# A planned attention-and-MLP kernel: more buffers lent to the Exp results, and a new plan

## The chip, the cores and the metric

The kernel runs on one core of a Trainium2 chip. The core has engines that work side by side and wait for each other through semaphores: TensorE (PE in the profile; its weight loads are PEld), VectorE (DVE), ScalarE (ACT), GpSimd (POOL) and SyncE (SP), which here issues the transfers. The metric is the device time of one execution in microseconds (us). The kernel before took 1624.14 us, the median of three runs (1622.63 to 1628.64). A further execution of it, which the hardware profiler recorded, took 1620.71 us; its trace spans 1618.9 us. Durations below are from that trace.

## The reference

Two layers are applied twice, with the same weights both times, to x of 2048 tokens by 512 features in bfloat16:

```python
def _A_ref(x, wqkv, wo):                     # 32 heads of 16 features
    qkv = (x @ wqkv) -> q, k, v per head
    p = softmax(q @ k.T * 16 ** -0.5)        # 2048 x 2048 for each head
    return concat_heads(p @ v) @ wo

def _B_ref(x, w1, w2):                       # 512 -> 1792 -> 512
    return silu(x @ w1) @ w2

for _ in range(2):
    x = x + _A_ref(layernorm(x), wqkv, wo)
    x = x + _B_ref(layernorm(x), w1, w2)
```

What costs most is the exponential of the scores: 2 layers x 32 heads x 2048 x 2048 values.

## The kernel before

**Tiles.** The tokens are four chunks c of 512 queries and sixteen blocks kt of 128 keys; the heads are eight head blocks hb of four heads. A segment (class Seg) is one layer, one chunk and one head block over a range of keys. There are 74 of them, numbered 0 to 73. Layer 1 (L = 0 in the code) has segments 0 to 31, all with 16 key blocks. In layer 2 the first two chunks begin before the last chunk of layer 1 has passed its MLP, so their head blocks are split: an "old" segment over the first 12 key blocks (numbers 32 to 41) and a "new" segment over the last 4 (among numbers 42 to 54). The old one's result is kept and is later multiplied by a factor and added to the new one's. A tile is two heads of a segment by one key block: 128 keys x 1024 scores. There are 2048 tiles, in a fixed order.

**What a tile passes through.** PE makes its scores (two products into one of three wide PSUM slots, `scores`). Then one of two ways follows. ACT takes the Exp of the whole tile into a buffer (`act_turn`), and PE multiplies that buffer with V (`values`). Or DVE makes an approximate power of two with one instruction (`dve_turn`, a "pass"), and three shifted copies of its bits are made, on POOL (`pool_turn`) or on DVE; PE then multiplies all four buffers with V. A pass thus takes one Exp off ACT and gives DVE one instruction, POOL or DVE three, and PE three more products with V. The buffers are 14 tiles p0 to p13 and, at times, rows of other tiles that are idle, which the list `lent` adds to the pool for a range of segments.

**Who decides the order.** Class Flow holds a clock for each engine with written-in durations, and steps through the kernel while it is built: at each step the engine that is first free takes its next instruction (`pe_turn`, `act_turn`, `dve_turn`, `pool_turn`). Engines execute in the order so written and do not reorder. Side work is cut into Pieces (K, Q, V, output projection, MLP) with due times. A letter for each 16 tiles (RULES) picks a row of KINDS: how many buffers must be free before a pass is chosen (`spare`), how many shifts may be queued, how hard side work is pushed, and so on; `want_dve` decides whether a tile goes to DVE. Where PE has nothing else and its planned share of the last 3300 ns is below WARM, `warm` issues a product with zero weights whose result adds nothing ("zero product", line 1393), to keep TensorE's clock up.

**The chain ahead of a segment.** Before a segment's first scores its QT must stand: the biased product q_ps on PE (`q_bias`, line 312), then `q_sum` on DVE (line 421). For layer 2's "new" segments a K piece goes ahead: four products, a copy to kq (line 334), `k_out` (line 321), a maximum (line 348) and the bias tile bm (line 412). When a segment ends, `close` copies its accumulated result (lines 1176, 1180 or 1184), a DMA transposes it, and `heads_norm` (lines 513 and 514) divides by the sums. A K or Q piece needs the one narrow PSUM bank, which the piece before it must have left.

Of the kernel before, what the change touches and what calls it, by code (L numbers as in the profile page):

```python
# [12 lines left out]
FP32 = mybir.dt.float32  # L13
# [7 lines left out]
def kernel(  # L21
# [14 lines left out]
    S, D = xf.shape  # L36
    F = B_w1.shape[-1]
    P = 128
    H = 32
    DH = D // H  # L40
# [3 lines left out]
    NQC = S // 512  # L44
    FT = F // P
    HB = H // 4
# [3 lines left out]
    VW = DH + 1  # L50
# [109 lines left out]
    E = cpool.tile([P, P], FP32, name="E")  # L160
# [104 lines left out]
    def dve(ns, fn, g=""):  # L265
        return ("dve", ns, fn, g)
# [62 lines left out]
    def k_piece(L, c, hb):  # L329
        cell = {}  # L330

        def out():
            st = cell["st"] = stpool.tile([P, 512], BF16, name="kq", tag="kq")
            nc.vector.tensor_copy(out=st[:], in_=cell["ps"][:, :])  # L334
            move(kept_q[L, hb, c, :, :], st[:])

        p = Piece(four(
            lambda cts: k_mm(c, hb, cell["ps"][:, :], cts),
            lambda: bank(cell, "k_ps"),
        ) + [dve(700, out, "c"), dve(302, lambda: k_out(c, hb, cell["st"][:]), "l")])  # L340
        p.key = (L, c, hb)
        p.store = Piece([])
        return p
# [163 lines left out]
        return fetch, f  # L507


    def heads_norm(at_ps, hb, attn):  # L510
        n = at_ps.shape[2]
        rec = bmpool.tile([P, 4, 8, 1], FP32, name="rec", tag="rec")[:, :, 0:n, :]
        nc.vector.reciprocal(rec, at_ps[:, :, :, DH : DH + 1])
        nc.vector.tensor_tensor(
            out=attn[:, :, 64 * hb : 64 * hb + DH * n].rearrange("p t (j d) -> p t j d", j=n),
            in0=at_ps[:, :, :, 0:DH],
            in1=rec.to_broadcast([P, 4, n, DH]),
            op=ALU.mult,
        )

# [2 lines left out]
    def heads_piece(oT, seg, attn):  # L523
        alone = seg.c < 2 and (seg.L == 1 or seg.hb < 2)
        alone = alone or (seg.L, seg.c, seg.hb) == (1, NQC - 1, HB - 2)
        k = 0 if alone else seg.hb % 2
        if k == 0:
            at_cell["at"] = opool.tile([P, 4, 2, P], BF16, name="at", tag="at")
        at = at_cell["at"]
        turn(at[:, :, k, :], oT[:])  # L530
        if not alone and k == 0:
            return None
        n = 4 * (k + 1)
        heads = at[:].rearrange("p t s (j w) -> p t (s j) w", j=4)[:, :, 0:n, :]
        return Piece([dve(640 if k == 0 else 920, lambda: heads_norm(heads, seg.hb - k, attn))])

    def o_transpose(a_ps, attn, tq):
        for ct in range(CT):
# [61 lines left out]
    def ffn_pieces(c, emit_out, ln, after):  # L600
# [33 lines left out]
            ))  # L634
        return pieces

    normed = {}

    def next_pieces(c, L, ln, after):
        ln = ln_pieces(c, ln, after)  # L640
        v = [v_piece(4 * c + tq, L) for tq in range(4)]
        normed[c] = ln[-1]
        v[0].after = [ln[-1]]
        return ln + v

    def tail_mm(slots, tq, k):
# [7 lines left out]
    def ending(oT, attn, slots, units):  # L654
# [27 lines left out]
        heads_norm(at_ps, hb, attn)  # L682
# [244 lines left out]
    done = n_old + 2 + 2 * HB  # L927
    keyed = max(s.i for s in segs if s.kind == "new" and s.c == 0) + 1
    lent = [
        (0, HB, spare(rows(x_flat, 0, 3))),  # L930
        (0, 2 * HB, spare(rows(x_flat, 3, 5))),
        (0, 3 * HB, spare(rows(x_flat, 5, 7))),
        (0, 4 * HB, spare(rows(x_flat, 7, 8))),
        (n_old + 3, n_old + HB, spare(idle_hidden)),
        (n_old + 4, 99, spare(wv_rows)),
        (keyed, 99, spare(key_rows)),
        (done, 99, spare(rows(v_flat, 0, 8))),
    ]

    class Flow:  # L940
# [36 lines left out]
        def rule(self, n):  # L977
            letter = RULES[n // STRETCH]
            (
                self.spare, self.many, self.few, self.behind, self.hurry, self.help, self.wait,  # L980
            ) = KINDS[letter]

        def landed(self, at):
# [184 lines left out]
        def close(self):  # L1168
# [17 lines left out]
            self.o_free = self.dve + 50  # L1186
            self.close_at = None
            self.open += 1
            if self.open == len(segs):
                return oT  # L1190
            if oT is not None:
# [54 lines left out]
            return max(self.end + 916 * (j + 1), t.at + 490 + 1017) + 50  # L1246

        def want_dve(self, t, at, two):
            if not two or t.n < 4 or t.n - self.last_dve < 2:
                return False  # L1250
            left = 2 * len(t.seg.kts) - 2 * (t.kt - t.seg.kts[0]) - t.pr
            if left < LAST or len(self.zs) > 0 or len(self.passes) > self.behind:
                return False
            if sum(b[0] <= at + 600 for b in self.bufs) - self.owed() < self.spare:
                return False
            if sum(len(l) for l in self.lanes) > ROWS:
                return False
            return self.dve < at + 475 + LATE
# [362 lines left out]
    KINDS = {  # L1621
# [10 lines left out]
    }  # L1632
# [161 lines left out]
```

## Time and profile before

| what | value |
|---|---|
| median of three runs | 1624.14 us (1622.63 to 1628.64) |
| profiled execution | 1620.71 us, span 1618.9 us |
| ACT | 1557.0 us busy, 1596 Exps in the flow |
| PE | 1546.3 us busy (matmul latency counted in) |
| DVE, POOL | 1239.8 us and 1293.6 us busy |
| DVE passes (line 1531) | 452 |
| zero products in the flow (line 1393) | 211 |
| granted TensorE clock, mean | 0.991 |

A busy PE in such a page is not a PE at its peak: a product's latency is counted with it, and 383 ns stand for one that others overlap. ACT's Exps overlap as well (a mean of about 1200 ns each, issued less than that apart), so its busy time is the time in which at least one ran. The line numbers are those of the kernel before.

### The profile page before, as it was taken

To read this page: it belongs to the slowest core of one execution; us is meant where nothing else is said; L and a number is where in the kernel's file an instruction comes from. 1 tells how busy PE (TensorE), PEld (TensorE's weight loads), DVE (VectorE), ACT (ScalarE), POOL (GpSimd) and SP (SyncE) were. 2 spreads that over 40 slices of the span, in tenths; PEclk is the share of its full clock that TensorE was granted. 3 is DMA by queue.
4 is the path that set the end of the run, shared out by engine and by line. 5 is a ranking of instruction groups with operands and counts; after the bars stand their busy time and mean duration, and the time that the engine had idled before them with its cause. 6 is when DMAs were issued, how large, how long until landed. Compare 5 with 4: busy or idle time off the path is not lost.

```text
span 1618.9 us, 41459 instructions
## 1 busy us (share of the span) xinstructions
PE 1546.3 (96%) x16750; PEld 477.4 (29%) x16756; DVE 1239.8 (77%) x1550; ACT 1557.0 (96%) x1767; POOL 1293.6 (80%) x1349
## 2 busy tenths in 40 slices
PE   8999999999999999999999999998999999999998
PEld 3322222233322323233222232222223222222333
DVE  7898888876777678658987668886878887777764
ACT  6999999999999999999999998998999999999993
POOL 3899998987898778868777866876879998889880
PEclk9999999999999999999999999998999999999999
DMA  5011101100210011001120011112100110010000
GB/s 195 21 40 37 30 23 27 27 11 11 37 23 11 11 27 41 11 14 33 57 59 23 14 27 35 37 35 45 30 11 17 33 27 14 18 33 18 17 24 14
DMA packets 105744, 49.24 MB, mean 30 GB/s; under 512 B 79024, under 2 KB 105040, under 8 KB 105552
## 3 DMA queue, kind: packets, MB, share of 16 engines
q1 hardware_dynamic: 103536, 45.51, 11.0%
q8 instruction: 131, 2.15, 0.6%
q10 hardware_dynamic: 2016, 1.08, 0.2%
q14 instruction: 61, 0.50, 0.1%
HBM read 17.20 MB, written 11.27 MB: 18 GB/s over the span
## 4 chain that ended last, share of the span: by engine, by line
PE 59%; ACT 22%; DVE 11%; issue 6%; POOL 2%; DMA 1%; ACTq 0%; DVEq 0%; POOLq 0%
PE slot L1282 21%; PE q_ps L1358 19%; ACT p L1497 15%; PE y_ps L312 7%; PE h_ps L312 4%; DVE p L1531 3%; ACT v L1497 3%; ACT t_sb L580 2%; PE k_ps L312 2%; PE v_ps L312 1%; PE q_ps L312 1%; POOL p L1592 1%; DVE hT L584 1%; PE w_ps L1393 1%; DVE kq L334 1%
## 5 line engine op out<-in xcount | busy, mean ns | idle before, releaser
L1497 ACT ACTIVATE p<-slot 128x1024 bf16<-128x1024 f32 x1168 | 1172.4, 1203 | 17.4 <-PE slot L1282 17.1
L1592 POOL TENSOR_TENSOR p<-p,steps 128x512 int32<-128x512 int32 x681 | 710.9, 1068 | 186.6 <-DVE p L1531 167.2
L1282 PE MATMUL slot<-QT,KT 32*128 32x512 bf16 x4096 | 596.6, 383 | 36.8 <-ACT p L1497 18.3
L1358 PE MATMUL q_ps<-p,v 128*17 128x512 bf16 x4956 | 566.1, 384 | 5.6 <-DVE p L1531 2.3
L1531 DVE TENSOR_SCALAR p<-slot 128x1024 uint16<-128x1024 f32 x341 | 415.5, 1219 | 106.0 <-PE slot L1282 99.9
L1282 PEld LDWEIGHTS <-KT 32*128 32x128 bf16 x4096 | 198.8, 91 | 615.9 <-issue 609.9
L1497 ACT ACTIVATE v<-slot 128x1024 bf16<-128x1024 f32 x289 | 329.3, 1211 | 1.9 <-PE slot L1282 1.9
L1358 PEld LDWEIGHTS <-v 128*17 128x17 bf16 x6808 | 157.3, 88 | 292.9 <-issue 244.1
L1358 PE MATMUL q_ps<-v,v 128*17 128x512 bf16 x1222 | 195.2, 382 | 1.2 <-POOL v L1592 0.8
L1592 POOL TENSOR_TENSOR v<-p,steps 128x512 int32<-128x512 int32 x159 | 170.4, 1081 | 23.2 <-DVE p L1531 17.1
L1592 POOL TENSOR_TENSOR p<-v,steps 128x512 int32<-128x512 int32 x123 | 130.8, 1081 | 8.4 <-DVE v L1531 8.0
L312 PE MATMUL h_ps<-xnT,w_sb 128*32 128x512 bf16 x1568 | 130.3, 384 | 6.8 <-DVE hT L584 6.6
L312 PE MATMUL y_ps<-w_sb,hT 128*32 128x512 bf16 x1568 | 121.8, 383 | 0.5 <-DVE hT L584 0.5
L584 DVE SCALAR_TENSOR_TENSOR hT<-t_sb,h_ps 128x512 bf16<-128x512 f32 x98 | 66.8, 682 | 58.2 <-ACT t_sb L580 57.9
L1531 DVE TENSOR_SCALAR v<-slot 128x1024 uint16<-128x1024 f32 x69 | 84.2, 1220 | 26.8 <-PE slot L1282 25.7
L1497 ACT ACTIVATE wkq<-slot 128x1024 bf16<-128x1024 f32 x74 | 87.2, 1215 | 0.1
L312 PE MATMUL k_ps<-xnT,wkq 128*32 128x512 bf16 x960 | 78.2, 383 | 0.0
L580 ACT ACTIVATE t_sb<-h_ps 128x512 f32<-128x512 f32 x98 | 76.0, 776 | 0.0
L421 DVE SCALAR_TENSOR_TENSOR QT<-qc,cols,q_ps 128x512 bf16<-128x512 bf16 x74 | 55.0, 743 | 21.6 <-PE q_ps L312 21.0
L1358 PE MATMUL q_ps<-wkq,v 128*17 128x512 bf16 x336 | 58.3, 387 | 0.6 <-ACT wkq L1497 0.4
L312 PEld LDWEIGHTS <-hT 128*32 128x32 bf16 x2016 | 41.0, 95 | 57.1 <-issue 40.8
L1497 ACT ACTIVATE wv_sb<-slot 128x1024 bf16<-128x1024 f32 x44 | 51.7, 1174 | 4.7 <-PE slot L1282 4.5
(168 smaller groups left out, 1469.5 us busy)
## 6 DMA issues: line engine op xcount, KB each, us to landing
qc<-kept_q SPq DMA_DIRECT2D x70, 112.0 KB, 2.0
kept_q<-kq SPq DMA_DIRECT2D x60, 128.0 KB, 1.8
w_sb<-in_B_w_dram SPq DMA_DIRECT2D x2, 1792.0 KB, 13.0
out_dram<-x_sb SPq DMA_DIRECT2D x15, 128.0 KB, 1.7
x_sb<-in_A_x_dram SPq DMA_DIRECT2D x3, 512.0 KB, 7.0
old_q<-QT SPq DMA_DIRECT2D x10, 128.0 KB, 1.7
q_was<-old_q SPq DMA_DIRECT2D x10, 128.0 KB, 2.0
at<-oT SPq DMA_TRANSPOSE x63, 2.3
```

The costliest lines, as they stand in the source:

```text
L312: nc.tensor.matmul(ps[g, :], lhsT=lhsT[:, g], rhs=rhs, start=start, stop=stop, skip_group_check=True)
L334: nc.vector.tensor_copy(out=st[:], in_=cell["ps"][:, :])
L421: nc.vector.scalar_tensor_tensor(out=dst, in0=qc[:], scalar=own, in1=ps, op0=ALU.mult, op1=ALU.add)
L580: nc.scalar.activation(t_sb, ps, ACT.Tanh, scale=0.5)
L584: nc.vector.scalar_tensor_tensor(out=hT[:, ft, :], in0=t_sb, scalar=1.0, in1=ps, op0=ALU.add, op1=ALU.mult)
L1282: nc.tensor.matmul(self.slots[k][:, jj, :], lhsT=KT[32 * j : 32 * j + KR, t.seg.hb, t.kt * P : (t.kt + 1) * P], rhs=t.seg.QT[32 * j : 32 * ...
L1358: nc.tensor.matmul(self.o_ps[32 * j : 32 * j + VW, :], lhsT=vs[seg.L][:, t.kt, 4 * seg.hb + j, :], rhs=buf[:, jj, :], start=not seg.opened ...
L1393: nc.tensor.matmul(out[0:DH, :], lhsT=wkq[rows, 0, 2 * D : 2 * D + DH], rhs=wo_sb[rows, 0, :], start=out is not self.o_ps, stop=out is not ...
L1497: nc.scalar.activation(buf[:].rearrange("p a b -> p (a b)"), self.slots[x.slot][:].rearrange("p a b -> p (a b)"), ACT.Exp, scale=float(SCALE),
L1531: nc.vector.tensor_scalar(out=whole.bitcast(U16), in0=self.slots[x.slot][:].rearrange("p a b -> p (a b)"), scalar1=float(UNIT), scalar2=fl ...
L1592: nc.gpsimd.tensor_tensor(out=b1.bitcast(I32), in0=b0.bitcast(I32), in1=steps32[:, k : k + 1].to_broadcast([P, 512]), op=ALU.add,)
```

## The change

1. **Lent buffers.** Rows of layer 2's V tile (x_flat) are lent during layer 1. Before, three, two, two and one buffers were taken back after segments 7, 15, 23 and 31. After, each chunk's V rows hold two buffers, taken back at segments 12, 20, 28 and 38, and a gate holds that chunk's V pieces until then. Rows of layer 1's V tile, which serve layer 2's kept results, are lent one by one while their result isn't yet written or is already used; before, all were lent from segment 59 on. Idle rows of the MLP's hidden tile are lent until segment 52 instead of 49.
2. **Planned durations ("clocks").** `k_out` is planned at 350 ns instead of 302. `heads_norm` is split into `heads_rec` and `heads_mul`, two steps with durations of their own, between which other work can stand.
3. **Zero products.** WARM goes from 0.65 to 0.70.
4. **Letters.** KINDS gets two more fields (`last`, `solo`, which `want_dve` reads), and RULES is written anew.

```diff
-        ) + [dve(700, out, "c"), dve(302, lambda: k_out(c, hb, cell["st"][:]), "l")])
+        ) + [dve(700, out, "c"), dve(350, lambda: k_out(c, hb, cell["st"][:]), "l")])
...
-        return Piece([dve(640 if k == 0 else 920, lambda: heads_norm(heads, seg.hb - k, attn))])
...
+        return Piece([dve(190 if k == 0 else 280, first), dve(410 if k == 0 else 560, second, "l")])
...
+    wanted = [HB * (c + 1) + HB // 2 for c in range(NQC - 1)] + [NQC * HB + HB - 2]
+    gates = [Piece([]) for c in range(NQC)]
...
-        v[0].after = [ln[-1]]
+        v[0].after = [ln[-1], gates[c]]
...
-        (0, HB, spare(rows(x_flat, 0, 3))),
-        (0, 2 * HB, spare(rows(x_flat, 3, 5))),
-        (0, 3 * HB, spare(rows(x_flat, 5, 7))),
-        (0, 4 * HB, spare(rows(x_flat, 7, 8))),
-        (n_old + 3, n_old + HB, spare(idle_hidden)),
+        *((0, wanted[c], spare(new_v_rows(c))) for c in range(NQC)),
+        *((99, NQC * HB + hb, old_o[hb]) for hb in range(1, HB)),
+        (n_old + 3, keyed - 1, spare(idle_hidden)),
         (n_old + 4, 99, spare(wv_rows)),
         (keyed, 99, spare(key_rows)),
-        (done, 99, spare(rows(v_flat, 0, 8))),
...
+            if self.open in wanted:
+                gate = gates[wanted.index(self.open)]
+                gate.done, gate.ready = True, self.pe
+            if seg.i == NQC * HB - 1:
+                self.bufs += [(self.pe, b) for hb in range(1, HB) for b in old_o[hb]()]
+            if seg.kind == "new" and seg.c == 0:
+                self.bufs += [(self.dve, b) for b in rows(v_flat, seg.hb, seg.hb + 1)()]
...
-            if not two or t.n < 4 or t.n - self.last_dve < 2:
+            if not two and len(self.exps) < self.solo or t.n < 4 or t.n - self.last_dve < 2:
...
-            if left < LAST or len(self.zs) > 0 or len(self.passes) > self.behind:
+            if left < self.last or len(self.zs) > 0 or len(self.passes) > self.behind:
...
-    LAST, ROWS, LATE, EVEN = 5, 20, 900, 0
-    SPAN, WARM = 3300, 0.65
+    ROWS, LATE, EVEN = 20, 900, 0
+    SPAN, WARM = 3300, 0.7
...
-        "bbbbbbbbmmmmmmmmwwwwwwwwwwwwwwwwppppppppbbbbbbbbddddddddcccccccc"
-        "aaaaaaaakkkkkkkknnnnnnnnvvvvvvvvwwwwwwwwwwwwwwwweeeeeeeellllllll"
+        "ggggggggggggggggllllllllaaaaaaaappppppppppppppppdddddddddddddddd"
+        "GGGGGGGGGGGGGGGGkkkkkkkkkkkkkkkknnnnnnnnnnnnnnnnaaaaaaaaaaaaaaaa"
```

No matrix product, Exp or transfer of the mathematics is added or left out; which tiles go to DVE, and the order on each engine, are.

More of the change, by code (lines that the diff above doesn't have):

```diff
@@ L507, in f_piece, with heads_rec, heads_mul @@
         return fetch, f
-    def heads_norm(at_ps, hb, attn):
-        n = at_ps.shape[2]
-        rec = bmpool.tile([P, 4, 8, 1], FP32, name="rec", tag="rec")[:, :, 0:n, :]
+    def heads_rec(at_ps):
+        m, n = at_ps.shape[1:3]
+        rec = bmpool.tile([P, 4, 8, 1], FP32, name="rec", tag="rec")[:, 0:m, 0:n, :]
         nc.vector.reciprocal(rec, at_ps[:, :, :, DH : DH + 1])
+        return rec
+    def heads_mul(at_ps, rec, hb, attn):
+        m, n = at_ps.shape[1:3]
         nc.vector.tensor_tensor(
@@ L516, in heads_norm @@
             in0=at_ps[:, :, :, 0:DH],
-            in1=rec.to_broadcast([P, 4, n, DH]),
+            in1=rec.to_broadcast([P, m, n, DH]),
             op=ALU.mult,
@@ L534, in heads_piece, with first, second @@
         heads = at[:].rearrange("p t s (j w) -> p t (s j) w", j=4)[:, :, 0:n, :]
-        return Piece([dve(640 if k == 0 else 920, lambda: heads_norm(heads, seg.hb - k, attn))])
+        cell = {}
+        def first():
+            cell["rec"] = heads_rec(heads)
+        def second():
+            heads_mul(heads, cell["rec"], seg.hb - k, attn)
+        return Piece([dve(190 if k == 0 else 280, first), dve(410 if k == 0 else 560, second, "l")])
     def o_transpose(a_ps, attn, tq):
@@ L681, in ending @@
         warm(max(0, 5 - len(units[4:])))
-        heads_norm(at_ps, hb, attn)
+        heads_mul(at_ps, heads_rec(at_ps), hb, attn)
         a_ps = gpool.tile([P, 4, P], BF16, name="a4_ps", tag="g")
@@ L925, in key_rows, with new_v_rows @@
         return [wkq[:, ct, 0 : 2 * D].rearrange("p (a b) -> p a b", a=2) for ct in range(CT)]
-    done = n_old + 2 + 2 * HB
     keyed = max(s.i for s in segs if s.kind == "new" and s.c == 0) + 1
+    def new_v_rows(c):
+        return rows(x_flat[:, 4 * H * VW * c : 4 * H * VW * (c + 1)], 0, 2)
+    old_o = [spare(rows(v_flat, hb, hb + 1)) for hb in range(HB)]
     lent = [
-        (0, HB, spare(rows(x_flat, 0, 3))),
-        (0, 2 * HB, spare(rows(x_flat, 3, 5))),
-        (0, 3 * HB, spare(rows(x_flat, 5, 7))),
-        (0, 4 * HB, spare(rows(x_flat, 7, 8))),
-        (n_old + 3, n_old + HB, spare(idle_hidden)),
+        *((0, wanted[c], spare(new_v_rows(c))) for c in range(NQC)),
+        *((99, NQC * HB + hb, old_o[hb]) for hb in range(1, HB)),
+        (n_old + 3, keyed - 1, spare(idle_hidden)),
         (n_old + 4, 99, spare(wv_rows)),
         (keyed, 99, spare(key_rows)),
-        (done, 99, spare(rows(v_flat, 0, 8))),
     ]
@@ L980, in rule @@
                 self.spare, self.many, self.few, self.behind, self.hurry, self.help, self.wait,
+                self.last, self.solo,
             ) = KINDS[letter]
```

21 rows, old and new, of the table KINDS are left out of this document.

## The prediction

> **What bounds the kernel now.** I read the page's engine table first, then the busy time of ACT by stretch, then who ACT waited for, and last the timelines of ACT and DVE around each of its waits.
>
> ```profile
> PE 1546.3 (96%) x16750; PEld 477.4 (29%) x16756; DVE 1239.8 (77%) x1550; ACT 1557.0 (96%) x1767; POOL 1293.6 (80%) x1349
> ...
> PEclk9999999999999999999999999998999999999999
> ```
>
> ACT and PE both stand at 96%. PE's figure counts latency; ACT decides, as the stretches show (start and end, length, ACT busy with its count, granted TensorE clock, DMA share, GB/s):
>
> ```profile
> 240.00:260.00 20.00, 18.48 (x20) 0.91 0.18 40
> 260.00:596.00 336.00, 335.58 (x381) 1.00 0.09 19
> 596.00:610.00 14.00, 12.97 (x15) 0.88 0.17 37
> 610.00:812.00 202.00, 202.00 (x228) 1.00 0.12 30
> ...
> 981.00:1000.00 19.00, 13.60 (x17) 1.00 0.14 41
> ...
> 1066.00:1092.00 26.00, 23.43 (x26) 0.87 0.19 36
> ...
> 1110.00:1142.00 32.00, 25.91 (x29) 0.79 0.22 40
> 1142.00:1540.00 398.00, 396.54 (x453) 1.00 0.10 22
> sum 1500.00, ACT 1477.19; mean ACT 113.63
> ```
>
> From 40 to 1540 us ACT is idle for 22.81 of 1500 us. Where the granted clock is full it hardly rests (0.42 of 336 us, 0 of 202, 1.46 of 398). It rests in four stretches whose clock is below 1.00, and at a few segment starts. The waits of that time go to one place, PE's scores; none goes to a missing buffer (waiter, whom for, us in total, times, longest):
>
> ```profile
> ACT p L1497 <- PE slot L1282: 15.2, 22, 4.0
> ACT wv_sb L1497 <- PE slot L1282: 4.5, 3, 3.5
> ACT v L1497 <- PE slot L1282: 1.9, 5, 0.6
> ```
>
> ACT's timeline has the single waits, in brackets, and the price of an Exp:
>
> ```profile
> 34.58 6.52 ACT L1497 ACTIVATE p<-slot 128x1024 bf16<-128x1024 f32 x7 [0.84 <-PE slot L1282]
> ...
> 813.83 2.85 ACT L1497 ACTIVATE p<-slot 128x1024 bf16<-128x1024 f32 x3 [1.08 <-PE slot L1282]
> ...
> 992.47 1.02 ACT L1497 ACTIVATE p<-slot 128x1024 bf16<-128x1024 f32 x1 [4.02 <-PE slot L1282]
> 999.94 5.61 ACT L1497 ACTIVATE p<-slot 128x1024 bf16<-128x1024 f32 x6 [1.38 <-PE slot L1282]
> ...
> 1121.88 1.02 ACT L1497 ACTIVATE wv_sb<-slot 128x1024 bf16<-128x1024 f32 x1 [3.53 <-PE slot L1282]
> ```
>
> A lone Exp takes 1.02 us and seven take 6.52, so one more costs (6.52 - 1.02) / 6 = 0.917 us. The waits at 813.83, 992.47, 999.94 and 1121.88 are the starts of segments 33, 43, 44 and 54: QT was late. DVE's timeline ahead of two of them:
>
> ```profile
> 983.99 1.22 DVE L1531 TENSOR_SCALAR p<-slot 128x1024 uint16<-128x1024 f32 x1
> ...
> 986.07 1.26 DVE L1565 TENSOR_SCALAR p<-p 128x1024 int16<-128x1024 int16 x1
> ...
> 1120.38 0.75 DVE L421 SCALAR_TENSOR_TENSOR QT<-qc,cols,q_ps 128x512 bf16<-128x512 bf16 x1 [3.41 <-PE q_ps L312]
> ```
>
> At segment 43 a pass and a shift stand in DVE's queue ahead of the K piece and QT; at 54 DVE waits 3.41 us for the biased product, at half the clock.
>
> **The change, part by part.** Counts come from the two programs' order of instructions on each engine.
>
> *Exps and passes.* Passes fall from 452 to 446, so ACT has 1602 Exps for 1596: 6 x 0.917 = **+5.5 us** on the engine that decides. POOL's shifts fall from 1203 to 1179, DVE's rise from 153 to 159, PE's products with V fall from 6808 to 6772. These lie beside ACT (DVE 77%, POOL 80% busy); if that cover went, they would be a gain.
>
> *Lent buffers.* No wait of ACT above is for a buffer, and passes don't rise, so more buffers alone are worth 0. The gate could hold V pieces, and behind them the K pieces of layer 2, but all V pieces stand in the same segments in both orders (16, 23 or 24, 30, 41): 0. If an Exp into a lent row had to wait for that row's last reader it would show as a new wait of ACT; by the list above the old lent rows cost at most 1.9 us in five waits, so 0 to +1.9, and I take 0, since all of those name the scores.
>
> *Late QTs.* I counted how many tiles of scores PE still has to issue after the biased product of the next segment. Most are far ahead; the close ones are the waits. Segment 43 keeps 0 tiles, but between QT of 42 and QT of 43 DVE loses one pass (1.22) and one shift (mean 0.77 in its rows): 2.0 us sooner, and ACT has one more Exp to fill with, so its idle time goes from 4.02 to 4.02 - 2.0 - 0.92 = 1.1: **-2.9**. The bounds are -4.0 (all of it) and 0 (the pass gone, but the K piece as late). Segment 44 likewise loses one pass and gains one Exp, 1.38 - 1.22 - 0.92 is below zero: **-1.4** (0 to -1.4). Segment 54's biased product comes two tiles earlier (0 to 2), and 55's too: 2 x 0.917 = -1.8, with 0.3 for 55: **-2.1** (0 to -3.5). Segment 33 gets worse: a kq copy (0.69), a `close` copy (0.69) and `k_out` (median 0.70) now stand ahead of its QT: **+2.1** on ACT's wait of 1.08 (0 to +2.9, with the K piece's 16 quarter products, 0.87, in full). Segment 2 goes from 1 tile to 0 and segment 73 from 11 to 1; the early segments with 0 (4, 6 and 8) show waits up to 0.3, hence **+0.6** for two (0 to +2.2, with segment 33's 1.08 each).
>
> *Zero products.* They go from 211 to 349. At about 0.22 us each that is 30 us of PE, but they're issued only where the plan has nothing else, and three slots stand between PE and ACT: 0, or up to 0.2 us where one delays a score pair at a late QT (a handful, +1). What they could bring is the clock. The four stretches below 1.00 hold 1.52 + 1.03 + 2.57 + 6.09 = 11.2 us of ACT idle, of which 4.0 (3.53 and 0.49 behind it) belongs to segment 54's QT. Of the other 7.2 I take half, **-3.6** (0 to -7.2): there are 65% more zero products in all, and 76 for 47 in segments 42 to 54, but in segment 24, which has the second stretch, 5 for 9.
>
> The Trainium skill's "TensorE: Matmul & The Clock Gate", section "What's actually happening", has the clock halve only after an idle window of about 3.4 us. In this trace PE was busy for 89% or more of each of the four stretches (28.62 of 32 us in the last), so it is not idleness in that sense that lowered the clock there. By that rule the zero products would be worth 0 and the sum 3.6 us higher.
>
> *The plan's durations, the split of `heads_norm`.* They act through the order alone: 43 reciprocals and 43 products in both, 0.29 and 1.03 us each. SP issues the same 316 instructions, DMAs among them, in both: 0.
>
> *The end.* In the kernel before, 16 quarter products of the output projection (four units) fill PE's gaps between the last products with V, from 1575.20 us on; after, the four come in the ending as whole products, (0.81 - 0.38) / 2 = 0.215 us each by the ending's run of three: **+0.9** (0 to +1.8).
>
> Sum: 5.5 - 2.9 - 1.4 - 2.1 + 2.1 + 0.6 - 3.6 + 0.9 = **-0.9 us** on an execution of 1620.71 us. That execution is 3.4 us below the median of 1624.14; the like step from the median gives **1623.2 us**.
>
> **The rivals.** *Paid in full (slower).* The Q chains at 43, 44 and 54 are not shortened: operations behind them (L404 and L412 from 0.28, L321 up to 1.31 us in their rows) fill the time of the pass. Then the 6.4 us of those terms don't come, and if the clock's share doesn't either, the sum is -0.9 + 6.4 + 3.6 = +9.1: **1633.2 us**. For it: `k_out` took 1.12 us at 988.24 where 0.41 is its least. Against it: ACT gets the Exps just where it was idle. It decides once ACT's idle time from 981 to 1142 us, 15.3 us before, stays within 1 us of that: then the sum passes 8.
>
> *The clock stays full (faster).* If no stretch falls below 1.00, the remaining 3.6 goes as well, the biased product of 54 isn't slowed (half of 3.41, 1.7), and the median's 3.4 above the profiled run, which I'd put down to more such stretches, goes too: 1623.2 - 8.7 = **1614.5 us**. For it: all big rests off segment starts stand in these stretches. Against it: the kernel before had zero products in them already.
>
> *Zero products don't touch the clock.* 1623.2 + 3.6 = **1626.8 us**, no change. A mechanism of its own: PE stays busy, yet the clock falls. The page named above is on this side.
>
> *The lending doesn't do what it says.* More buffers, and fewer passes: this is what the counts show, and it is in the sum.
>
> **How the numbers follow.** A measurement of this kernel can tell about 0.5%, 8 us, from no change. My forecast, 1623.2, has 0.47; zero products without effect 0.10; the full clock 0.25; paid in full 0.18. So faster 0.25, same 0.57, slower 0.18. The first two lie between 1619.6 (all 7.2 of the clock) and 1626.8 (none of it). The range for 8 in 10 reaches into both outer cases: 1611 (beyond the full clock's 1614.5 by the -3.5 that segment 54 may bring at most) to 1633, which leaves out about 1 in 10 on each side.
>
> **What would show it.** ACT's Exps (line 1519 in the changed code) number 1602, still at 0.917 us. ACT's wait at segment 33 is near 3 us, at 43 near 1, at 44 gone, at 54 under 2. The stretches below 1.00 number two or three for four. From the last `close` (at 1576.99) to the end it was 41.9 us; 0.9 more is expected. I am wrong if ACT waits in places where QT is early, above all for lent rows, or if the clock's stretches multiply in spite of the zero products.

## The result: slower by half a per cent

The changed kernel takes 1632.91 us, the median of 15 runs (1625.67 to 1637.74); the kernel before, run beside it, 1622.63 us (15 runs, 1619.67 to 1629.24). The ratio of the two is 1.005, with a 95% interval of 1.0035 to 1.0066: about 8 us slower (the medians of these two sets lie 10.3 us apart), where 1623.2 and no change were forecast.

The profiled execution of the changed kernel took 1625.67 us and spans 1623.9. It is the quickest of the 15. Every run lists its span and its mean granted clock; the profiled one had 0.991, the median of the 15 is 0.985. So this profile shows the changed kernel on a good day, and a second one, taken later, shows an ordinary run.

Its page, with the engines' busy time and the granted clock in 40 slices:

```profile
PE 1565.7 (96%) x16840; PEld 486.0 (30%) x16846; DVE 1223.0 (75%) x1550; ACT 1563.2 (96%) x1773; POOL 1269.8 (78%) x1325
...
PEclk9999999999999999999999999999999999999999
```

ACT has six instructions more and 6.2 us more busy time; DVE and POOL have less. Whom ACT waited for from 40 to 1560 us (waiter, whom for, us in total, times, longest):

```profile
ACT p L1519 <- PE slot L1304: 12.3, 16, 3.2
ACT v L1519 <- PE slot L1304: 2.8, 6, 0.8
ACT v L1519 <- POOL idle L1614: 1.2, 1, 1.2
```

With the small rows that are not shown, the waits for scores fell from 22.2 to 15.9 us. One is new in kind: an Exp into a lent row of the V tile at 1094.29 us is put down to a shift on POOL. ACT's timeline has its waits at the starts of segments 33, 42 and 43, then the nine Exps among which segment 44 starts (at 1008.09 us), and the first Exp of segment 54:

```profile
819.85 1.94 ACT L1519 ACTIVATE p<-slot 128x1024 bf16<-128x1024 f32 x2 [3.20 <-PE slot L1304]
...
991.52 2.85 ACT L1519 ACTIVATE p<-slot 128x1024 bf16<-128x1024 f32 x3 [0.82 <-PE slot L1304]
...
1000.94 1.02 ACT L1519 ACTIVATE p<-slot 128x1024 bf16<-128x1024 f32 x1 [2.40 <-PE slot L1304]
...
1002.33 8.62 ACT L1519 ACTIVATE p<-slot 128x1024 bf16<-128x1024 f32 x9
...
1127.38 1.07 ACT L1519 ACTIVATE p<-slot 128x1024 bf16<-128x1024 f32 x1
```

Segment 33 waits 3.20 us (1.08 before), 43 waits 2.40 (4.02), segment 44 has no wait (1.38) and 54 none (3.53). Segment 42, which did not wait before, now does for 0.82 us. The chains ahead of the segments moved much as the order of instructions said. What did not go as forecast stands in ACT's busy time by stretch (start and end, length, ACT busy with its count, granted clock, DMA share, GB/s):

```profile
240.00:300.00 60.00, 57.67 (x64) 0.94 0.13 31
...
414.00:424.00 10.00, 7.57 (x8) 0.66 0.18 39
424.00:812.00 388.00, 387.39 (x437) 1.00 0.10 26
...
972.00:984.00 12.00, 10.83 (x12) 0.86 0.08 19
...
1066.00:1092.00 26.00, 24.79 (x28) 0.91 0.15 40
1092.00:1110.00 18.00, 16.73 (x20) 0.94 0.09 29
1110.00:1142.00 32.00, 31.80 (x36) 1.00 0.22 53
...
1460.00:1474.00 14.00, 12.41 (x14) 0.88 0.26 39
```

The stretch from 1110 to 1142 us is whole again, but the clock falls in six places for four, with new ones at 286 to 300, at 414, at 972 and at 1466 us. ACT rests 10.0 us in these rows (2.33 + 2.43 + 1.17 + 1.21 + 1.27 + 1.59; the fourth and fifth share one fall). Without the wait of 1.17 us for a lent row it is 8.8, against the 7.2 us that the prediction set beside segment 54's own 4.0 before. In the first profiles of the two kernels the time at half the clock is nearly the same: about 28 us in each, by their mean clock of 0.991.

The second profile, of the same program in a run of 1636.01 us, has more of the same: ten falls of the clock. PE in three stretches there (PE busy with its count, then the granted clock):

```profile
410.00:430.00 20.00, 19.66 (x154) 0.74 0.18 41
530.00:550.00 20.00, 18.98 (x205) 0.83 0.05 14
...
750.00:770.00 20.00, 19.73 (x144) 0.74 0.15 34
```

And in the first profile:

```profile
410.00:430.00 20.00, 19.63 (x168) 0.83 0.21 47
530.00:550.00 20.00, 18.98 (x229) 1.00 0.05 14
...
750.00:770.00 20.00, 19.67 (x227) 1.00 0.12 27
```

At 750 us both are at the same place of the order, to within some 30 products. Over the 20 us that follow PE is busy for 98% in both, and in the one the clock is full, in the other 0.74. PE got 144 products done instead of 227. ACT's timeline of the ordinary run shows the price, a rest of half a us before nearly every Exp, in the middle of a segment, where the first profile has 15 Exps without one:

```profile
757.26 1.02 ACT L1519 ACTIVATE v<-slot 128x1024 bf16<-128x1024 f32 x1 [0.48 <-PE slot L1304]
...
761.07 1.02 ACT L1519 ACTIVATE p<-slot 128x1024 bf16<-128x1024 f32 x1 [0.48 <-PE slot L1304]
762.55 1.02 ACT L1519 ACTIVATE p<-slot 128x1024 bf16<-128x1024 f32 x1 [0.46 <-PE slot L1304]
```

**Where the 8 us are.** In the traces the clock is full or half, nothing between. A fall lasts 3.41 us, or two, three or four times that. So a run spent h = 2 x (1 - mean clock) x span at half the clock: 49 us in the median run of the changed kernel, 36 in that of the kernel before (over its 82 runs beside the experiments below). A straight line through the runs gives 1615.3 + 0.36 h for the changed kernel (15 runs) and 1613.4 + 0.32 h for the one before; the two starting values are uncertain by 0.8 and 0.5 us. At the full clock the change would cost 1.9 us. The other 0.36 x 49 - 0.32 x 36 = 6.1 us is clock. With one slope for both kernels, 0.33, the split is 3.8 and 4.4 us. So the clock has 4 to 6 of the 8 us.

### The profile page after: what moved, and what is told of

Its sections match the earlier page's. It is cut to its first block, busy times and chain, and to the rows that moved or that the text cites. A ratio compares the mean times of both kernels' runs of the same rounds, so it can differ in the third digit from the quotient of the medians.

```text
span 1623.9 us, 41563 instructions
## 1 busy us (share of the span) xinstructions
PE 1565.7 (96%) x16840; PEld 486.0 (30%) x16846; DVE 1223.0 (75%) x1550; ACT 1563.2 (96%) x1773; POOL 1269.8 (78%) x1325
## 3 DMA queue, kind: packets, MB, share of 16 engines
q10 hardware_dynamic: 2016, 1.08, 0.2%
## 4 chain that ended last, share of the span: by engine, by line
PE 61%; ACT 20%; DVE 10%; issue 6%; POOL 2%; DMA 1%; ACTq 0%; DVEq 0%; SPq 0%; POOLq 0%
PE slot L1304 22%; PE q_ps L1380 19%; ACT p L1519 11%; PE y_ps L312 7%; ACT v L1519 4%; PE h_ps L312 4%; PE k_ps L312 3%; ACT t_sb L592 2%; DVE p L1553 2%; PE q_ps L1415 2%; POOL p L1614 1%; DVE v L1553 1%; DVE hT L596 1%; PE w_ps L1415 1%; PE q_ps L312 1%
## 5 line engine op out<-in xcount | busy, mean ns | idle before, releaser
L1519 ACT ACTIVATE p<-slot 128x1024 bf16<-128x1024 f32 x1069 | 1091.8, 1199 | 15.3 <-PE slot L1304 14.3
L1614 POOL TENSOR_TENSOR p<-p,steps 128x512 int32<-128x512 int32 x489 | 513.3, 1069 | 151.4 <-DVE p L1553 127.5
L1519 ACT ACTIVATE v<-slot 128x1024 bf16<-128x1024 f32 x400 | 452.0, 1197 | 4.6 <-PE slot L1304 2.8
L1553 DVE TENSOR_SCALAR p<-slot 128x1024 uint16<-128x1024 f32 x280 | 341.7, 1220 | 111.4 <-PE slot L1304 103.1
L1380 PE MATMUL q_ps<-v,v 128*17 128x512 bf16 x1726 | 274.6, 383 | 1.3 <-DVE v L1553 0.5
L1614 POOL TENSOR_TENSOR p<-v,steps 128x512 int32<-128x512 int32 x218 | 229.6, 1070 | 41.1 <-DVE v L1553 34.2
L1614 POOL TENSOR_TENSOR v<-p,steps 128x512 int32<-128x512 int32 x194 | 207.4, 1079 | 37.2 <-DVE p L1553 34.7
L1553 DVE TENSOR_SCALAR v<-slot 128x1024 uint16<-128x1024 f32 x131 | 159.8, 1220 | 51.3 <-PE slot L1304 41.9
L1614 POOL TENSOR_TENSOR v<-v,steps 128x512 int32<-128x512 int32 x85 | 90.7, 1073 | 24.9 <-DVE v L1553 22.7
L1415 PE MATMUL q_ps<-wo_sb,wkq 128*16 128x512 bf16 (+1 forms) x267 | 92.8, 384 | 0.0
```

The costliest lines, as they stand in the source:

```text
L1380: nc.tensor.matmul(self.o_ps[32 * j : 32 * j + VW, :], lhsT=vs[seg.L][:, t.kt, 4 * seg.hb + j, :], rhs=buf[:, jj, :], start=not seg.opened ...
L1415: nc.tensor.matmul(out[0:DH, :], lhsT=wkq[rows, 0, 2 * D : 2 * D + DH], rhs=wo_sb[rows, 0, :], start=out is not self.o_ps, stop=out is not ...
L1519: nc.scalar.activation(buf[:].rearrange("p a b -> p (a b)"), self.slots[x.slot][:].rearrange("p a b -> p (a b)"), ACT.Exp, scale=float(SCALE),
L1553: nc.vector.tensor_scalar(out=whole.bitcast(U16), in0=self.slots[x.slot][:].rearrange("p a b -> p (a b)"), scalar1=float(UNIT), scalar2=fl ...
L1614: nc.gpsimd.tensor_tensor(out=b1.bitcast(I32), in0=b0.bitcast(I32), in1=steps32[:, k : k + 1].to_broadcast([P, 512]), op=ALU.add,)
```

## The experiments

My theory after the result: the plan of the changed kernel spreads PE's useful work worse, more windows have too little of it, and the zero products that were to hold the clock there don't do it. Rivals: the zero products themselves take the time (PE does 138 more); the lending or the letters bring late QTs or waits for buffers, and the clock only goes along; the clock differs from batch to batch by chance. Each kernel is compared with the kernel before of its own batch, whose median was 1622.92, 1625.21, 1624.59 and 1626.98 us in turn. "Us at half the clock" is h as above.

### Without zero products

The products that do nothing are left out in the flow, everything else keeps its place (in the changed kernel 349, in the one before 211):

```diff
-            nc.tensor.matmul(
-                out[0:DH, :], lhsT=wkq[rows, 0, 2 * D : 2 * D + DH], rhs=wo_sb[rows, 0, :],
-                start=out is not self.o_ps, stop=out is not self.o_ps, skip_group_check=True,
-            )
             self.pe = t + MM
```

> The changed kernel with its plan kept instruction for instruction, but the 349 zero products of the flow left out (they add nothing to the result). My theory: the changed kernel is slower by two things, six Exps more (5.5 us) and more time at half the TensorE clock in the typical run. Over its 15 runs the time follows the granted clock: 0.991 goes with 1625.7 us, 0.982 with 1637.7, that is 0.36 us for each us at half clock. If the zero products hold the clock up, leaving them out drops the mean granted clock well below 0.985, to 0.96 or less, and the time rises by 20 us or more over the changed kernel. Rival: zero products don't count for the clock; then the clock stays within 0.003 of the changed kernel's and the time within 4 us of it.

Measured: 1635.88 us (four runs), ratio 1.0082 (1.005 to 1.0115), clock 0.972, so 92 us at half the clock. The clock fell, as the theory said, but less far, and the 20 us did not come: a miss.

> The kernel before, plan kept, its 211 zero products left out. In the changed kernel leaving out 349 lowered the median clock from 0.985 to 0.972 (42 us more at half clock, 12 to 15 us by the slope) yet cost only 3 us, so the zero products themselves cost some 10 us, 0.03 us each. By that, here: clock 0.975 to 0.985, and the time within 4 us of before: 211 x 0.03 = 6 us saved against 20 to 40 us more at half clock (6 to 14 us). Rival: zero products are free; then the time rises by the clock's loss alone, by 10 us or more.

Measured: 1622.65 us (ten runs), ratio 0.9986 (0.9966 to 1.0005), clock 0.984, 52 us at half the clock.

Without fillers the changed kernel has 92 us at half the clock and the kernel before 52. That is what the order of the useful work does alone, and it is the largest difference between the two. The zero products do lift the clock (92 to 49 us, 52 to 36), so "zero products don't touch the clock" falls. But they bring no time: neither kernel gets measurably slower without them. The lines through these runs meet the full clock at 1608.6 and 1605.7 us, some 7 to 8 us under the same kernels with zero products, so these cost about what they earn: 0.02 to 0.04 us each (6.7 / 349 and 7.7 / 211). This is an estimate from lines carried far beyond their runs; the first of them, through four runs, is uncertain by about 6 us.

### WARM and the letters by themselves

```diff
-    SPAN, WARM = 3300, 0.65
+    SPAN, WARM = 3300, 0.7
```

> The kernel before with WARM 0.70 and nothing else. The new plan has 1589 Exps (7 fewer: -6.4 us) and 401 zero products in the flow for 211. If zero products hold the clock, its clock is above the before's and the time is 1616 us or less beside a before of 1622.6. If they don't, the clock is no better than the before's, and the time is 1616 plus or minus what the clock's chance gives. Rival (each zero product delays a score pair): slower than before in spite of fewer Exps.

Measured: 1658.41 us, ratio 1.0223 (1.0192 to 1.0255), at a clock of 0.9905. Seven Exps fewer and nearly twice the zero products, and some 35 us slower: a miss. ACT waits 17.5 us for the scores of segment 42.

The reverse in the changed kernel, 0.7 to 0.65:

> The changed kernel with WARM back at 0.65. The plan has 1605 Exps (3 more than the changed kernel: +2.8 us) and 241 zero products in the flow for 349. If zero products hold the clock, the granted clock is lower than the changed kernel's and the time is above 1636 us. If they don't, clock as the changed kernel's, 1636 us. If zero products cost time by themselves, under 1633.

Measured: 1630.03 us (ten runs), ratio 1.0036 (1.002 to 1.0053), clock 0.9905, 31 us at half the clock. With 241 zero products for 349 the clock is better, not worse, than in the changed kernel, against the theory; but the order of all other work has changed with it. At the full clock this kernel would take 1620.6, 5 us more than the changed one. WARM changes the plan before it changes the clock.

The new KINDS and RULES, and `last`, in the kernel before:

> The kernel before with the letters alone renewed (KINDS, RULES, the field last); lending, durations and WARM as before. The plan has 1601 Exps, 5 more than before (+4.6 us), and 258 zero products for 211. If the letters carry the loss: 1627 us or more beside 1622.6, the clock deciding how much more. If the lending, the gate or the durations carry it, the time is within 4.6 us of before with the clock equal.

Measured: 1634.43 us (six runs), ratio 1.0066 (1.0044 to 1.0089), at a clock of 0.9915.

### Lending, planned durations, and all but the letters

The lending with its gate, alone in the kernel before (the lines of the change's first part):

> The change's lending alone (per chunk, with the gate), with the old clocks and letters. The orders of instructions give 1589 Exps (7 fewer than before, 7 x 0.917 = -6.4 us of ACT) and 306 zero products for 211 in the flow and the end. Theory (more buffers alone don't touch the starts of the segments, but the more zero products, 16 columns wide, cost some 0.03 us each, and the letters no longer fit the plan): ACT's idle time between 40 and 1560 us rises by at least what the seven Exps were worth, 1620 to 1632 us. Rival 1 (lending is what makes the changed kernel slow): ACT waits for buffers, the waits on the chain of time name something other than the scores, over 1632. Rival 2 (fewer Exps are paid out in full): 1616 to 1619.

Measured: 1656.37 us, ratio 1.0199 (1.0174 to 1.0225). Seven Exps fewer, and 32 us slower, above the theory's range. In ACT's waits nearly all is for scores (waiter, whom for, us, times, longest):

```profile
ACT p L1506 <- PE slot L1291: 49.6, 27, 17.5
```

The longest is the first segment of layer 2's new keys, number 42 (ACT's timeline):

```profile
995.49 2.85 ACT L1506 ACTIVATE p<-slot 128x1024 bf16<-128x1024 f32 x3 [0.32 <-PE slot L1291]
1015.81 2.85 ACT L1506 ACTIVATE p<-slot 128x1024 bf16<-128x1024 f32 x3 [17.46 <-PE slot L1291]
```

DVE's timeline shows what it waited for. Layernorm's last step for the chunk began at 994.55 us (at 959.75 in the kernel before), then four V pieces, the K piece and QT came in a row, with PE and DVE waiting for each other:

```profile
994.55 2.49 DVE L227 TENSOR_SCALAR hT<-x_sb,sc 128x512 bf16<-128x512 bf16 x3
...
1008.80 0.69 DVE L379 CAST v<-v_ps 128x512 bf16<-128x512 f32 x1 [1.15 <-PE v_ps L312]
1010.73 0.69 DVE L334 CAST kq<-k_ps 128x512 bf16<-128x512 f32 x1 [1.24 <-PE k_ps L312]
...
1014.52 0.75 DVE L421 SCALAR_TENSOR_TENSOR QT<-qc,cols,q_ps 128x512 bf16<-128x512 bf16 x1 [1.42 <-PE q_ps L312]
```

The last Exp of the old segments ended at 998.3 us, so they were used up when this chain had only begun. No wait of more than 0.3 us is for a buffer, so the rival that ACT waits for buffers falls.

The planned durations and the split of the normalisation, alone:

```diff
...
-        return Piece([dve(640 if k == 0 else 920, lambda: heads_norm(heads, seg.hb - k, attn))])
...
+        return Piece([dve(190 if k == 0 else 280, first), dve(410 if k == 0 else 560, second, "l")])
...
```

> The change's planned durations and the split of the heads' normalisation alone, with the old lending and letters. The orders give 1600 Exps (4 more, +3.7 us) and 301 zero products. Theory (the durations act through the order alone; the old letters were fitted to the old durations): +3.7 us and late QTs that the old letters don't cure, 1627 to 1636 us, at a clock between 0.98 and 0.99. Rival (the durations themselves place the QT chains better, and idle time falls by as much as the Exps cost): 1619 to 1625.

Measured: 1653.9 us, ratio 1.0206 (1.0164 to 1.0249), clock 0.9905; above what I had expected. ACT waits 48.4 us for scores, the longest, 8.8 and 8.5, at segments 55 and 42.

The changed kernel with the letters of before (new lending, durations and WARM):

> The changed kernel with the letters of before: lending and clocks new, letters old. The orders give 1591 Exps and 490 zero products. Lending alone gave 1656, clocks alone 1654, letters alone 1634. Theory (the letters are fitted to one plan, and any other plan meets late QTs): 1645 to 1665 us, with ACT's idle time between 40 and 1560 us at 45 to 60 us. Rival (letters are good or bad by themselves, and the new ones are the worse, as the run with them alone could be read): under 1633.

Measured: 1679.87 us, ratio 1.0319 (1.0293 to 1.0346), slower than I expected. Two waits of 22 us and more, at segments 33 and 42 (waiter, whom for, us, times, longest):

```profile
ACT p L1519 <- PE slot L1304: 44.9, 25, 22.6
ACT v L1519 <- PE slot L1304: 32.4, 14, 22.0
```

So the parts don't add up. From the kernel before, lending costs 32 us by itself, the durations 29, WARM 35 and the letters 12, and all together 8. Each of the first three shifted the plan under letters fitted to another, and made QTs late by up to tens of us; new letters take that back (1679.87 us with the old ones, 1632.91 with the new). "Late QTs explain the changed kernel's loss" falls, though: in the changed kernel they are taken back (ACT's waits for scores are 6 us less than before), and at least half of what remains is clock.

### The changed kernel once more

No edit, a second profile.

> The changed kernel once more, for a second profile: the first fell on the fastest of 15 runs (clock 0.991 where the median is 0.985). My theory: the extra 20 us at half clock of the typical run lie in stretches where the first profile was already near the limit (290, 412, 816, 1084, 1461 us), in longer chains of cold windows. Rival: they lie anywhere, or the typical run's time is not lost at cold windows but in waits elsewhere.

Measured: 1636.05 us (four runs), ratio 1.0064 (1.004 to 1.0087); the profiled run had 0.982. Its rows are shown above. Of the places that I had named, the clock fell for longer at 412 us alone (10.2 us for 6.8). The falls at 538, 756 and 1057 us are at places that I had not named, so on where they lie the rival was nearer. Over two batches the changed kernel was slower by the same half per cent, so chance between batches is out.

### Zero products of 128 columns

The zero products stay where they are, but each takes 128 columns of zero weights (one zero column repeated) for 16:

```diff
-                out[0:DH, :], lhsT=wkq[rows, 0, 2 * D : 2 * D + DH], rhs=wo_sb[rows, 0, :],
+                out[0:P, :], lhsT=wkq[rows, 0, 2 * D : 2 * D + 1].to_broadcast([rows.stop, P]),
+                rhs=wo_sb[rows, 0, :],
```

> The kernel before, plan unchanged, each of its 211 zero products widened from 16 to 128 columns of zero weights (still 512 columns long). In six profiles the windows of 3.41 us ahead of a fall of the clock are told best from the others by useful PE time plus half the zero products' time, with a limit near 0.5. If a zero product counts little because it fills few of the array's columns, widening makes it count in full: the median clock rises from 0.991 to 0.995 or more, and the time falls by 3 to 8 us (29 us at half clock, 0.28 to 0.36 us each). Rival: it counts little because its numbers are zero, or for another reason; then clock 0.991 and time as before within 2 us.

Measured: 1621.51 us (ten runs), ratio 0.9969 (0.9952 to 0.9985), clock 0.993.

> The changed kernel with its 349 zero products widened from 16 to 128 columns, plan unchanged. If columns count: the median clock rises from 0.985 to 0.993 or more and the time from 1632.9 to 1623 to 1627 us, with what is left over the kernel before being the six Exps. Rival: clock 0.985, 1633 us.

Measured: 1621.37 us (ten runs), ratio 0.9988 (0.9966 to 1.0011), clock 0.9955, 15 us at half the clock.

This is the run that decides. The plan is the changed kernel's, instruction for instruction, and 11.5 us of its median are gone (14.7 beside the narrow products in the same batch). A line through its runs meets the full clock at 1615.0 us, where that of the narrow ones has 1615.3, so it is the clock that the edit changed. PE in the same three stretches:

```profile
410.00:430.00 20.00, 19.50 (x223) 1.00 0.28 60
530.00:550.00 20.00, 19.32 (x222) 0.83 0.06 14
...
750.00:770.00 20.00, 19.36 (x246) 1.00 0.09 23
```

The two worst stretches are whole. The product itself is hardly longer (line, engine, operation and count; min, median and max ns; first and last start; forms). In the first profile of the changed kernel:

```profile
L1415 PE MATMUL q_ps<-wo_sb,wkq x267: 374/379/631, 70.4 to 1533.4; 128*16 128x512 bf16 x116, 32*16 32x512 bf16 x18
```

and with 128 columns (the trace has lost some of the records):

```profile
L1415 PE MATMUL q_ps<-wo_sb,wkq x179: 372/389/392, 70.7 to 1498.9; 128*128 128x512 bf16 x144, 32*128 32x512 bf16 x35
```

379 and 389 ns. Its weight load goes from 86 to 95 ns (median of 349 each). With the clock held, the changed kernel and the one before differ by 0.1 us in their medians, or by 0.0019 in their ratios (3.1 us) with intervals that overlap. The changed one has the better clock of the two; their lines meet the full clock at 1615.0 and 1612.4 us.

### Fewer and wider

If wide products hold the clock and each costs a little, fewer should do. The plan stays; a wide zero product is issued only where PE's planned share of the last window, the issued ones counted in, is under a limit, here 0.6:

```diff
+            self.pe = t + MM
+            self.runs.append((t, self.pe))
+            self.unmade = [r for r in self.unmade if r[1] > t - SPAN]
+            if self.share(t) - sum(b - max(a, t - SPAN) for a, b in self.unmade) / SPAN > 0.6:
+                self.unmade.append((t, self.pe))
+                return True
...
-                out[0:DH, :], lhsT=wkq[rows, 0, 2 * D : 2 * D + DH], rhs=wo_sb[rows, 0, :],
+                out[0:P, :], lhsT=wkq[rows, 0, 2 * D : 2 * D + 1].to_broadcast([rows.stop, P]),
...
```

> The kernel before, the plan's order of all other work unchanged; the 211 narrow zero products become 63 of 128 columns, issued only where PE's planned busy share of the last window, those issued included, is under 0.6. Zero products give nothing that the result needs. Theory (a wide product counts for the clock in full, a narrow one by about a half, and each product costs PE some 0.02 to 0.04 us wherever it stands): the clock stays at 0.990 or above and some 150 products less are paid, 1612 to 1619 us, faster than with all 211 wide (1621.5). Rival 1 (it is the number of fillers that holds the clock): the clock falls to 0.984 as with none, 1621 to 1625. Rival 2 (fillers cost nothing): as with all wide, 1620 to 1623.

Measured: 1616.66 us (twelve runs), ratio 0.9957 (0.9942 to 0.9971), clock 0.993. This one beats both kernels. (The counts 63, 116, 239, 146, 371 and 233 in these expectations include 22 products of the ending; 211 and 349 do not.)

> The same edit of the changed kernel: the 349 narrow zero products become 116 of 128 columns, the ending's included, everything else in its order. Theory as for the kernel before: a clock of 0.990 or above and some 230 products less, 1612 to 1620 us, faster than with all of them wide (1621.4). Rival 1 (the number of fillers holds the clock): 0.97 as with none, 1630 to 1637. Rival 2 (fillers cost nothing): 1620 to 1623.

Measured: 1625.83 us (twelve runs), ratio 1.0007 (0.9991 to 1.0024), clock 0.986. A miss: the clock was not held. PE at one place where it fell:

```profile
800.00:820.00 20.00, 18.02 (x187) 0.92 0.26 74
820.00:840.00 20.00, 19.38 (x176) 0.74 0.04 13
```

With a limit of 0.7, 239 fillers for 116:

> The changed kernel with 239 wide zero products (where the planned share is under 0.70) for 116 (under 0.60) and 371 (all). Theory (the plan's clock for PE runs away from the real one by more than a window, so the places with little work must be filled with a margin; the clock is the only thing missing): 0.992 to 0.996, 1616 to 1621 us, below both other fillings. Rival (it takes all 371, the places can't be told from the plan): 0.987 to 0.990, 1622 to 1626.

Measured: 1619.85 us (twelve runs), ratio 0.9959 (0.9944 to 0.9974), clock 0.9925. The places can be told from the plan, with more margin in the changed kernel.

> The kernel before with 146 wide zero products (under 0.70) for 63 (under 0.60) and 233 (all). At 63 the clock was 0.993 already, as with all of them. Theory (each filler that doesn't lift the clock costs 0.02 to 0.04 us): between the two, 1617 to 1621 us. Rival (fillers are free where PE has nothing else, the gain of the sparse ones was their clock): 1614 to 1616.

Measured: 1619.16 us (five runs), ratio 0.9951 (0.9932 to 0.997), clock 0.992. Its interval overlaps that of 63 fillers, so whether 83 fillers cost anything can't be told from this run. Over all fillings the lines meet the full clock later the more fillers there are: at 1608.6, 1611.6, 1612.2 and 1615.0 us in the changed kernel (none, 116, 239 and 371 in that count). This fits a price of some 0.02 us for each.

In this last batch the changed kernel with wide fillers and the kernel before with wide fillers stand 0.7 us apart. What the lending, the durations and the letters did to the work is a draw to within 2 to 4 us; the clock made the rest.

## Why the prediction was wrong

The step that failed is the one on the zero products: -3.6 us, "of the other 7.2 I take half", argued from 65% more zero products. In the profiled execution the rests beside the half clock rose from 7.2 to 8.8 us; over the runs the clock's share is +4.4 to +6.1 us (by the lines above). So that term was wrong in sign and by 8 to 10 us, and neither of its bounds, 0 and -7.2, lay on the side where the truth was. Two things were not asked. One is what the new order does to PE's useful work: without fillers it has 92 us at half the clock, where the old order has 52. The other is why the clock had fallen in spite of zero products already there; the prediction named this as an argument against "the clock stays full", and did not follow it. The text's own sign of error came true: "the clock's stretches multiply in spite of the zero products", six in the first profile for the two or three that it gave. That 1632.91 still lies at the very end of the range, 1611 to 1633, is luck: that end was drawn for "paid in full", which did not happen.

Without that term the sum was -0.9 + 3.6 = +2.7 us. The lines of the runs give +1.9 to +3.8 at the full clock, and the first profile, with the same clock of 0.991 as the profile of before, +5.0 (1623.9 - 1618.9). That the rest of the sum came out so well is in part luck, since terms were off in opposite directions (segments 43 and 54 below).

Point by point, in the first profile of the changed kernel:

- Six more Exps, +5.5: right, 1602 of them, at the same price (2.85 us for three, so (2.85 - 1.02) / 2 = 0.915 for one more).
- Lent buffers, 0 (up to 1.9): one wait of 1.17 us into a lent row, inside the bounds.
- Segment 33, +2.1 on 1.08: right, 3.20.
- Segments 2 and 73, +0.6: 0.41 at 2 and none at 73. The 0.82 at segment 42 was not forecast.
- Segment 44, -1.4: right, no wait.
- Segment 43, to 1.1: it is 2.40, so -1.6 for -2.9. The pass and the shift did go. But of the 2.0 us that this was to save between the two QTs 0.9 came (10.30 us from QT to QT before, 9.42 after). DVE's timeline shows what took the place. The multiplication of a kept old result by its factor (L496) and the sum that a `close` makes (L1180, now L1195) stood in the queue before too. But with the pass gone DVE came to L496 before the factor was there, and waited 1.56 us for ACT's `f_sb`. Before:

```profile
985.12 1.02 DVE L496 TENSOR_TENSOR v<-v,f_sb 128x512 f32<-128x512 f32 x1
...
990.58 0.68 DVE L1180 TENSOR_TENSOR oT<-v,q_ps 128x512 bf16<-128x512 f32 x1
991.18 0.74 DVE L421 SCALAR_TENSOR_TENSOR QT<-qc,cols,q_ps 128x512 bf16<-128x512 bf16 x1
```

After:

```profile
994.90 1.50 DVE L496 TENSOR_TENSOR v<-v,f_sb 128x512 f32<-128x512 f32 x1 [1.56 <-ACT f_sb L493]
996.32 0.68 DVE L334 CAST kq<-k_ps 128x512 bf16<-128x512 f32 x1
...
999.01 0.69 DVE L1195 TENSOR_TENSOR oT<-v,q_ps 128x512 bf16<-128x512 f32 x1
999.61 0.74 DVE L421 SCALAR_TENSOR_TENSOR QT<-qc,cols,q_ps 128x512 bf16<-128x512 bf16 x1
```

- Segments 54 and 55, -2.1 (0 to -3.5): more came. ACT rested 6.09 us from 1110 to 1142 and now 0.20. The clock is full there in this execution, and other runs tell the two causes apart. In the order of the kernel before with the clock full at that place, segment 54 waits 1.63 us (wide zero products) or 0.65 (sparse wide ones, with either limit) for 3.53, so 1.9 to 2.9 us of it were the clock. The new order took the rest: no trace of it with the changed kernel's plan has a wait there.
- The end, +0.9: from the last `close` (at 1580.84) to the end of the span 43.0 us for 41.9, so +1.1.
- The step from the profiled run to the median, 3.4 us in both: wrong. It is 7.2 in the changed kernel (1632.91 - 1625.67), whose profiled run was the quickest of the 15. One profiled run of such a kernel says too little on its own.

The rivals. "Paid in full" gave 1633.2 us, and 1632.91 came; yet it is refuted. Its condition was that ACT's 15.3 us of rest from 981 to 1142 stay; from 984 to 1142 us, about the same segments, ACT was busy for 151.87 of 158 us, a rest of 6.1, and almost none of it at the chains of 44 and 54. At segment 43 its mechanism did show in part: half of the time that the pass gave free was filled by a wait. A right number is no proof of its mechanism. "The clock stays full" did not happen; the run with wide fillers, at 0.9955, came within 7 us of its 1614.5. "Zero products don't touch the clock" is refuted by the kernels without them.

The Trainium skill's "TensorE: Matmul & The Clock Gate", section "What's actually happening", has the clock halve after an idle window of about 3.4 us. The window's length agrees: the falls in these traces last 3.41 us or a multiple of it. An idle PE does not: from 750 to 770 us PE was busy for 19.73 of 20 us at a clock of 0.74, so the measurement decides: PE need not be idle, as a profile's row counts it, for the clock to halve.

## What to carry to other kernels

Before crediting fillers with a clock, work out how the change spreads the useful work over windows as long as a fall of the clock (here 3.4 us), and ask what the fillers there now have failed to do. In a kernel whose order is planned with fitted letters, an edit of the plan can't be priced alone: three parts that cost 29 to 35 us each came to 8 together with letters fitted to them. Where the clock varies from run to run, read the clock of every run beside its time before comparing two profiles.

## What the runs showed of the hardware

A product with 16 columns of weights takes nearly as long as one with 128 (379 and 389 ns) and reads as busy just the same, but holds the clock less well: going from 16 to 128 columns took the mean clock from 0.985 to 0.9955 in the changed kernel (from 0.989 to 0.993 in the other) with all weights still zero. So the columns in use count there, and weights of zero don't keep a product from counting. Whether other values would count for more, no run tested.

What the clock goes by can be fitted, but not pinned down. In ten of these traces (both profiles of the changed kernel, that of the kernel before, and those without zero products, with all of them wide, with the other WARM and with the new letters alone) there are 63 falls of the clock between 40 and 1566 us, and some 4300 windows of 3.41 us after which it stayed full. Take PE's time in each window as 0.2 us a product (about the step from one zero product to the next where they come in a row), or less where the next one starts sooner, and leave out a share of the narrow zero products' time. With half of it left out, the share of busy time is smaller ahead of a fall than ahead of no fall in 98.9% of the pairs; with none left out in 97.7%, with all in 98.2%. But if each product is given its 0.2 us in full, the three are 99.1, 99.3 and 98.9%, and the half is no longer the best. So the fit says that the clock falls after windows with little work (62 of the 63 shares are 0.54 or less, but so are some 230 of the others), and it doesn't settle what a narrow product counts for. No run tested that weight or a limit by itself. Why the changed kernel at a limit of 0.6 lost its clock at 820 us, where PE was busy for 19.38 of 20 us, stays open. A us at half the clock costs this kernel about a third of a us (the slopes above); it would be half a us if all the time hung on PE.
